# Background conversion's transfers issued from GpSimd, its steps spread by one, and attention's places in a tile changed

## The chip, the cores and the metric

The kernel runs on one core of a Trainium2 chip. The metric is the device time in microseconds of one execution. Three executions of the kernel before gave 1234.53, 1236.09 and 1236.2 us, median 1236.09. A fourth one was taken with the profiler: 1233.03 us, of which 1230.9 us lie between its first and last recorded instruction (the span). All rows below come from that one.

## The reference

Chunked attention with memory tokens, then two feed-forward layers; all in float32.

```python
def _attn_ref(q, k, v, mem_k, mem_v):          # (4, 8, 768, 64), chunks of 32, window 16 back, 8 ahead, 8 memory rows
    for c in range(nc):
        k_full = concat([mem_k, k[l_start:r_end]]); v_full = concat([mem_v, v[l_start:r_end]])
        scores = scale * q_c @ k_full.T
        a = exp(scores - max(scores)); a = a / (sum(a) + 1e-09)
        out[c] = a @ v_full

def _moe_ref(x, w_gate, w_val, w_out, rms_g):   # 3072 tokens, 512 -> 1536 -> 512
    xn = x / sqrt(mean(x * x) + 1e-06) * rms_g
    return (silu(xn @ w_gate) * (xn @ w_val)) @ w_out

def _moe2_ref(x, w_in, w_out):                  # 512 -> 2048 -> 512
    h = x @ w_in
    g = where(h >= 1, h, where(h <= -1, 0, (h + 1) ** 2 / 4))
    return g @ w_out
```

The weights come to the chip as 64-bit floats. The kernel makes float32 of them with integer operations and splits each value into a high and a low part, so that a product is three matmuls: high by high, high by low, low by high.

## The kernel before, in words

The 3072 tokens are six tiles of 512. The program has these stages, by the profile's clock:

- **Start** (to 38 us): attention for the first tokens, in an order written out by hand.
- **Tile 0 of the first layer** (to about 152 us): proj_in (L519) makes gate and value for one block f of 128 hidden columns, out1 (L540) multiplies the block before into ps_y. The first layer's weights are converted beside it, the low parts on GpSimd.
- **Tiles 1 to 3** (to about 530 us): the same loop over f = 0 to 11. Every f has three slots (L689); a slot is one step of attention for later tokens, perhaps one step of preparing the pair, and two steps of a background list `bg`. After this point the order of all instructions on all engines is the program's own.
- **Tiles 4 and 5 as a pair** (about 530 to 720 us): seven products per block instead of eight (product, L807; proj1, L830) in the banks b1 to b4, and out1p (L927). A step of `bg` follows every product, and two follow out1p (L975).
- **Second layer** (720 us to the end): three pairs of tiles, proj2 and out2. No background work is left here.

The list `bg` (L300 to L302) has two kinds of step. w1_steps (L203) makes four sums and differences of quarter blocks of the first layer's weights and stores their high and low parts to DRAM, for the pair. w2_steps (L237) does the conversion for the second layer, in eight groups of four 512-KB blocks a, b, o0 and o1: load_w2 (L232) loads one, c (L245) takes the upper words on ScalarE (ACT), d (L249, three operations of join, L128) makes the float32 on VectorE (DVE), hi (ACT) and lo (DVE) split it, and store (L263) writes it to DRAM; hi_s, lo_s and store_s (L192 to L201) do the same for the sums s1234. Loaded blocks and sums share three buffers in turn (wst, L72), so a load waits until the store that read its buffer has landed. In the kernel before all these loads and stores are issued by ACT: `nc.scalar.dma_start` at L200, L201, L235 and L265. Each engine takes its instructions in order, so a DMA issue that waits holds what stands behind it on the issuing engine.

Attention in tiles 1 to 3 is laid out by `plan2` (L646): which of nine steps of one pair of units stands in which slot; pairs follow each other by 11 slots. A step's name is its kind and its half: s is the scores (matmuls into the bank pair ps_a, then maximum and subtraction on DVE and the exponential on ACT), a the transposes of the exponentials into ps_a and their copy to the tile aT on ACT (part_A, L405), v the product with the values (step_v, L411; DVE then scales it into x_nat), r the normalisation of the rows by the factor rs, which GpSimd raises to a power (part_p, L475), x the transposes of x_nat and their copy on ACT (part_X, L496), whose result xn goes to DRAM as x_d (L506). xn is taken from the same single buffer "aT" that part_A uses.

Of the kernel before, what the change touches and what calls it, by code (L numbers as in the profile page):

```python
# [8 lines left out]
F32 = mybir.dt.float32  # L9
F32R = mybir.dt.float32r  # L10
BF16 = mybir.dt.bfloat16
U32 = mybir.dt.uint32
# [4 lines left out]
P = 128  # L17
# [21 lines left out]
def tile_stream_attention_moe_moe2(  # L39
# [10 lines left out]
    nc = tc.nc  # L50
# [3 lines left out]
    KK = DM // P  # L54
# [8 lines left out]
    att = att_only.enter_context(tc.tile_pool(name="att", bufs=1, side="right"))  # L63
# [119 lines left out]
    def sums(S, a, b, first):  # L183

        if first:
            tt_(out=S[:, 0], in0=b[0], in1=b[1], op=ALU.add)
            tt_(out=S[:, 2], in0=a[0], in1=b[0], op=ALU.subtract)
        else:
            tt_(out=S[:, 1], in0=S[:, 0], in1=a[0], op=ALU.subtract)
            tt_(out=S[:, 3], in0=a[1], in1=S[:, 1], op=ALU.subtract)  # L190

    def hi_s(S, k, h):  # L192
        nc.scalar.activation(h.bitcast(F32R), flat(S[:, k:k + 2]), AF.Copy)

    def lo_s(S, k, h):
        sk = flat(S[:, k:k + 2])
        tt_(out=sk, in0=sk, in1=h.bitcast(F32), op=ALU.subtract)

    def store_s(S, k, h, dp):
        nc.scalar.dma_start(flat(dp[:, 0, 3 + k:5 + k]), h.bitcast(F32))  # L200
        nc.scalar.dma_start(flat(dp[:, 1, 3 + k:5 + k]), flat(S[:, k:k + 2]))  # L201

    def w1_steps(f):  # L203
        g, v = wall[:, 3 * f].bitcast(F32), wall[:, 3 * f + 1].bitcast(F32)
        dp = w1p_d[f]
        st = {}
        half_ = lambda n: [st[n].bitcast(F32)[:, k:k + 256] for k in (0, 256)]

        def whole():
            nc.sync.dma_start(dp[:, :, 0:2].rearrange("p h k c -> p h (k c)"), g)  # L210
            nc.sync.dma_start(dp[:, :, 2], v[:, :, 256:512])
            nc.sync.dma_start(w1o_d[f], wall[:, 3 * f + 2].bitcast(F32))
            for n, w in (("g", g), ("v", v)):
                st[n] = tmp.tile([P, 512], U32, tag="tu", name="w" + n)
                tt_(out=st[n].bitcast(F32), in0=w[:, 0], in1=w[:, 1], op=ALU.add)

        def first():
            st["s"] = wst.tile([P, 4, 256], F32, tag="w64", name="s1234")
            sums(st["s"], half_("g"), half_("v"), True)

        yield whole
        yield first
        yield lambda: sums(st["s"], half_("g"), half_("v"), False)
        yield lambda: hi_s(st["s"], 0, st["g"])
        yield lambda: lo_s(st["s"], 0, st["g"])
        yield lambda: (store_s(st["s"], 0, st["g"], dp), hi_s(st["s"], 2, st["v"]))
        yield lambda: lo_s(st["s"], 2, st["v"])
        yield lambda: store_s(st["s"], 2, st["v"], dp)

    w2raw = {}  # L230

    def load_w2(i):  # L232
        if i < 2 * F2:
            w2raw[i] = wst.tile([P, 1024], U32, tag="w64", name="w64")
            nc.scalar.dma_start(w2raw[i], wts2[i].bitcast(U32))  # L235

    def w2_steps(g):  # L237
        a, b, o0, o1 = 4 * g, 4 * g + 2, 4 * g + 1, 4 * g + 3
        dp, do = w2p_d[g], w2o_d[g]
        f32_, st = {}, {}  # L240
        A = lambda i: [f32_[i].bitcast(F32)[:, k:k + 256] for k in (0, 256)]

        part = lambda i, n: w2raw[i][:, 512 * n:512 * n + 512]

        def c(i):  # L245
            f32_[i] = tmp.tile([P, 512], U32, tag="tu", name="tu")
            nc.scalar.activation(f32_[i].bitcast(F32), words(w2raw[i])[1].bitcast(F32), AF.Copy, scale=2.0 ** -112)

        def d(i):  # L249
            join(f32_[i], w2raw[i])  # L250

        def hi(i, n=0):
            nc.scalar.activation(part(i, 0)[:, n:].bitcast(F32R), f32_[i].bitcast(F32)[:, n:], AF.Copy)

        def lo(i, n=0):
            tt_(
                out=part(i, 1)[:, n:].bitcast(F32),
                in0=f32_[i].bitcast(F32)[:, n:],
                in1=part(i, 0)[:, n:].bitcast(F32),
                op=ALU.subtract,  # L260
            )

        def store(i, dst, n=0):  # L263
            src = w2raw[i].bitcast(F32).rearrange("p (h c) -> p h c", h=2)
            nc.scalar.dma_start(dst, src[:, :, n:])  # L265

        def first():
            st["s"] = wst.tile([P, 4, 256], F32, tag="w64", name="s1234")
            sums(st["s"], A(a), A(b), True)

        if g == 0:
            yield lambda: load_w2(a)
            yield lambda: load_w2(b)
            yield lambda: None
        yield lambda: c(a)
        yield lambda: d(a)
        yield lambda: (hi(a), load_w2(b) if g else None)
        yield lambda: lo(a)
        yield lambda: store(a, dp[:, :, 0:2].rearrange("p h k c -> p h (k c)"))
        yield lambda: None  # L280
        yield lambda: c(b)
        yield lambda: d(b)
        yield lambda: (hi(b, 256), first())
        yield lambda: lo(b, 256)
        yield lambda: (store(b, dp[:, :, 2], 256), sums(st["s"], A(a), A(b), False))
        yield lambda: (hi_s(st["s"], 0, f32_[a]), load_w2(o0))
        yield lambda: lo_s(st["s"], 0, f32_[a])
        yield lambda: (store_s(st["s"], 0, f32_[a], dp), hi_s(st["s"], 2, f32_[b]), load_w2(o1))
        yield lambda: lo_s(st["s"], 2, f32_[b])
        yield lambda: store_s(st["s"], 2, f32_[b], dp)  # L290
        yield lambda: c(o0)
        yield lambda: d(o0)
        yield lambda: (c(o1), load_w2(4 * g + 4))
        yield lambda: (d(o1), hi(o0))
        yield lambda: lo(o0)
        yield lambda: (store(o0, do[:, :, 0]), hi(o1))
        yield lambda: lo(o1)
        yield lambda: store(o1, do[:, :, 1])

    bg = [st for f in range(F1) for st in w1_steps(f)]  # L300
    bg += [st for g in range(G2) for st in w2_steps(g)]
# [27 lines left out]
    x_t = {}  # L329
# [166 lines left out]
    def part_X(pr, blk):  # L496
        t, o = divmod(pr, 2)
        ps = ps_t.pop(("x", pr, blk))
        c0 = (2 * o + blk) * P
        if t < 2:  # L500
            xn = xn_t[t][:, :, c0:c0 + P]
        else:
            xn = att.tile([P, KK, P], F32, tag="aT", name="xn")
        nc.scalar.activation(xn, ps[:, 0, :].rearrange("p (k i) -> p k i", k=KK), AF.Copy)
        if t >= 2:
            nc.sync.dma_start(x_d[t][:, :, c0:c0 + P], xn)  # L506
# [136 lines left out]

    plan2 = {0: "s0", 2: "a0", 3: "v0", 4: "s1", 6: "a1", 7: "v1", 9: "r0", 10: "x0", 12: "x1"}  # L646

    def att_slot(t, s):
        if t == 0:
# [34 lines left out]
    def conv_step(n):  # L684
        for _ in range(n):
            if bg:
                bg.pop()()
# [283 lines left out]
    for f in range(F1):  # L971
        proj1(f)
        if f:
            out1p(0, [f - 1])
        conv_step(2)  # L975
        if f == 6:
            load_y(y_d[0], y_d[1])
    out1p(0, [F1 - 1])
# [117 lines left out]
```

## Time and profile before

| what | value |
|---|---|
| median of three executions | 1236.09 us |
| the profiled execution, its span | 1233.03 us, 1230.9 us |
| TensorE (PE) busy | 1172.4 us, 95% of the span |
| DVE, ACT, GpSimd (POOL) busy | 760.8, 501.9, 86.2 us |
| mean granted TensorE clock | 0.986 of full speed |
| HBM traffic | 225 GB/s over the span |

A page of the profile gives one execution. "Idle before" an instruction is the time in which its engine had nothing running, and the releaser is what ended it. ACTq, SPq and POOLq are the queues from which an engine issues DMAs; an issue is not counted as busy time. The granted clock is the share of full TensorE speed that the throttle allowed.

### The profile page before, as it was taken

Reading aid. Unit: us, or ns where it says so; the run is one execution under the profiler, and the core shown is the slowest. Engines: PE = TensorE matmul, PEld = TensorE weight load, DVE = VectorE, ACT = ScalarE, POOL = GpSimd, SP = SyncE. Lnnn points to the kernel's source line nnn. Section 1 sums busy time; section 2 is a strip of 40 time slices with the busy share of each in tenths; the row PEclk is TensorE's granted clock in tenths of the full one; section 3 lists DMA queues with packets and bytes.
Section 4 is the critical chain, followed back from the end, with each engine's and each line's share of the span. In section 5 each row is a group of like instructions: output and inputs, shape, how many; then the busy total and the mean of one; then the engine's idle time right before and its main releaser. Section 6 shows DMA issues by size and latency. Waiting matters only on the chain.

```text
span 1230.9 us, 19786 instructions
## 1 busy us (share of the span) xinstructions
PE 1172.4 (95%) x7993; PEld 941.1 (76%) x7993; DVE 760.8 (62%) x1256; ACT 501.9 (41%) x830; POOL 86.2 (7%) x75
## 2 busy tenths in 40 slices
PE   6888999998999999988999999999999999999998
PEld 4666777776777778866777788888888888888887
DVE  5898856666546665866766537666267664366630
ACT  4656554445445563533333314334133332233320
POOL 2555510000000000000000000000000000000000
PEclk8989999999999999998999999999999999999999
DMA  8564547777756666498786667657655756565354
GB/s 295 179 196 164 181 157 279 266 276 276 261 179 227 212 202 231 158 348 309 297 338 243 221 220 258 252 192 250 209 200 197 271 194 234 184 235 188 128 183 158
DMA packets 106699, 278.57 MB, mean 226 GB/s; under 512 B 8944, under 2 KB 22256, under 8 KB 100208
## 3 DMA queue, kind: packets, MB, share of 16 engines
q1 hardware_dynamic: 78320, 218.59, 50.8%
q10 hardware_dynamic: 28288, 58.73, 13.2%
q8 instruction: 62, 1.02, 0.3%
q14 instruction: 29, 0.24, 0.1%
HBM read 209.13 MB, written 68.16 MB: 225 GB/s over the span
## 4 chain that ended last, share of the span: by engine, by line
PE 74%; DVE 9%; DMA 9%; ACT 4%; issue 3%; ACTq 1%; POOL 0%; SPq 0%; DVEq 0%; POOLq 0%
PE ps_y L950 7%; PE ps_y L951 7%; PE ps_y L952 7%; PE ps_g L515 5%; PE ps_g L517 5%; PE ps_g L516 5%; PE ps_b L814 5%; PE ps_b L816 5%; PE ps_b L815 5%; PE ps_y L515 4%; PE ps_y L516 4%; PE ps_y L517 4%; PE ps_g L814 3%; PE ps_g L815 3%; PE ps_g L816 3%
## 5 line engine op out<-in xcount | busy, mean ns | idle before, releaser
L515 PE MATMUL ps_g<-xh,wall 128*128 128x512 f32 x384 | 158.4, 412 | 0.0
L517 PE MATMUL ps_g<-xh,wall 128*128 128x512 f32 x384 | 152.7, 398 | 0.0
L516 PE MATMUL ps_g<-xl,wall 128*128 128x512 f32 x384 | 152.6, 397 | 0.0
L950 PE MATMUL ps_y<-wo,wall 128*128 128x512 f32 x324 | 126.2, 389 | 0.3 <-DMA wo<-w2o_d 0.3
L951 PE MATMUL ps_y<-wo,wall 128*128 128x512 f32 x324 | 126.1, 389 | 0.0
L952 PE MATMUL ps_y<-wo,wall 128*128 128x512 f32 x324 | 126.0, 389 | 0.0
L874 ACT ACTIVATE t<-t,half 128x512 f32<-128x512 f32 x96 | 69.0, 720 | 131.5 <-DVE t L873 131.5
L814 PE MATMUL ps_b<-wall 128*128 128x512 f32 x288 | 114.0, 396 | 7.2 <-DVE p L846 7.2
L815 PE MATMUL ps_b<-wall 128*128 128x512 f32 x288 | 113.1, 393 | 0.0
L816 PE MATMUL ps_b<-wall 128*128 128x512 f32 x288 | 113.1, 393 | 0.0
L814 PE MATMUL ps_g<-wall 128*128 128x512 f32 x216 | 85.2, 394 | 7.7 <-ACT p L840 5.6
L888 DVE TENSOR_TENSOR t<-t,ps_g 128x512 f32<-128x512 f32 x24 | 16.5, 688 | 113.5 <-PE ps_g L816 108.8
L517 PEld LDWEIGHTS ps_g<-xh,wall 128*128 128x128 f32 x384 | 72.9, 190 | 17.7
L515 PEld LDWEIGHTS ps_g<-xh,wall 128*128 128x128 f32 x384 | 73.2, 191 | 17.2
L516 PEld LDWEIGHTS ps_g<-xl,wall 128*128 128x128 f32 x384 | 73.3, 191 | 15.4
L816 PE MATMUL ps_g<-wall 128*128 128x512 f32 x216 | 84.7, 392 | 0.0
L815 PE MATMUL ps_g<-wall 128*128 128x512 f32 x216 | 84.6, 392 | 0.0
L515 PE MATMUL ps_y<-hh,wall 128*128 128x512 f32 x192 | 79.1, 412 | 2.6 <-ACT hh L105 2.6
L516 PE MATMUL ps_y<-hl,wall 128*128 128x512 f32 x192 | 76.7, 400 | 0.2 <-DVE hl L106 0.2
L517 PE MATMUL ps_y<-hh,wall 128*128 128x512 f32 x192 | 76.5, 398 | 0.0
L950 PEld LDWEIGHTS ps_y<-wo,wall 128*128 128x128 f32 x324 | 60.8, 188 | 13.4 <-DMA wo<-w2o_d 0.8
L814 PEld LDWEIGHTS ps_b<-wall 128*128 128x128 f32 x288 | 54.7, 190 | 21.0 <-DVE p L846 9.7
(146 smaller groups left out, 2222.0 us busy)
## 6 DMA issues: line engine op xcount, KB each, us to landing
wo<-w2o_d SPq DMA_DIRECT2D x100, 512.0 KB, 4.9
wall<-w2p_d SPq DMA_DIRECT2D x24, 1792.0 KB, 7.2
wall<-w1p_d SPq DMA_DIRECT2D x12, 1792.0 KB, 7.9
w<-in_w_dram SPq DMA_DIRECT2D x36, 512.0 KB, 4.0
w<-in_w_dram ACTq DMA_DIRECT2D x32, 512.0 KB, 4.7
v_in<-in_v_dram SPq DMA_DIRECT2D x48, 260.0 KB, 4.1
k_in<-in_k_dram SPq DMA_DIRECT2D x48, 256.0 KB, 4.3
wo<-w1o_d SPq DMA_DIRECT2D x24, 512.0 KB, 5.7
```

Of the source, the lines that this page charges most:

```text
L515: nc.tensor.matmul(ps, wh, xh, start=start, stop=False)
L516: nc.tensor.matmul(ps, wh, xl, start=False, stop=False)
L517: nc.tensor.matmul(ps, wl, xh, start=False, stop=stop)
L814: nc.tensor.matmul(bank, wh, xh, start=st, stop=False, skip_group_check=True)
L815: nc.tensor.matmul(bank, wh, xl, start=False, stop=False, skip_group_check=True)
L816: nc.tensor.matmul(bank, wl, xh, start=False, stop=kk == 1, skip_group_check=True)
L874: nc.scalar.activation(s, s, AF.Square, scale=0.5, bias=half)
L888: tt(out=u2, in0=a, in1=b2, op=ALU.add)
L950: nc.tensor.matmul(ps_y[m], hi[:, sl], wh, start=b == 0, stop=False)
L951: nc.tensor.matmul(ps_y[m], hi[:, sl], wl, start=False, stop=False)
L952: nc.tensor.matmul(ps_y[m], lo[:, sl], wh, start=False, stop=b == F2 - 1)
```

## The change

Three edits.

1. The transfers of `bg` (store_s, load_w2, store) are issued by GpSimd instead of ACT, and the lists of steps are dealt anew: a step of one engine is mostly followed by a free step before the next engine's, and a store stands in the step of its own lo. w1_steps has 7 steps per block instead of 8, a group of w2_steps 28 instead of 24. In the pair's stage one step follows out1p instead of two.
2. part_X writes xn over the rows' own tile x_nat instead of into a buffer of aT.
3. In plan2 s1 moves from slot 4 to 3, v0 from 3 to 4 and a1 from 6 to 5.

```diff
     def store_s(S, k, h, dp):
-        nc.scalar.dma_start(flat(dp[:, 0, 3 + k:5 + k]), h.bitcast(F32))
-        nc.scalar.dma_start(flat(dp[:, 1, 3 + k:5 + k]), flat(S[:, k:k + 2]))
+        nc.gpsimd.dma_start(flat(dp[:, 0, 3 + k:5 + k]), h.bitcast(F32))
+        nc.gpsimd.dma_start(flat(dp[:, 1, 3 + k:5 + k]), flat(S[:, k:k + 2]))
...
         yield lambda: hi_s(st["s"], 0, st["g"])
-        yield lambda: lo_s(st["s"], 0, st["g"])
-        yield lambda: (store_s(st["s"], 0, st["g"], dp), hi_s(st["s"], 2, st["v"]))
-        yield lambda: lo_s(st["s"], 2, st["v"])
-        yield lambda: store_s(st["s"], 2, st["v"], dp)
+        yield lambda: hi_s(st["s"], 2, st["v"])
+        yield lambda: (lo_s(st["s"], 0, st["g"]), store_s(st["s"], 0, st["g"], dp))
+        yield lambda: (lo_s(st["s"], 2, st["v"]), store_s(st["s"], 2, st["v"], dp))
...
-            nc.scalar.dma_start(w2raw[i], wts2[i].bitcast(U32))
+            nc.gpsimd.dma_start(w2raw[i], wts2[i].bitcast(U32))
...
-            nc.scalar.dma_start(dst, src[:, :, n:])
+            nc.gpsimd.dma_start(dst, src[:, :, n:])
...
         yield lambda: c(a)
+        yield none
         yield lambda: d(a)
-        yield lambda: (hi(a), load_w2(b) if g else None)
-        yield lambda: lo(a)
-        yield lambda: store(a, dp[:, :, 0:2].rearrange("p h k c -> p h (k c)"))
-        yield lambda: None
-        yield lambda: c(b)
+        yield none
+        yield lambda: (c(b), hi(a))
+        yield none
         yield lambda: d(b)
-        yield lambda: (hi(b, 256), first())
-        yield lambda: lo(b, 256)
-        yield lambda: (store(b, dp[:, :, 2], 256), sums(st["s"], A(a), A(b), False))
+        yield lambda: (lo(a), sa())
+        yield lambda: hi(b, 256)
+        yield first
+        yield lambda: (lo(b, 256), sb())
+        yield lambda: sums(st["s"], A(a), A(b), False)
         yield lambda: (hi_s(st["s"], 0, f32_[a]), load_w2(o0))
-        yield lambda: lo_s(st["s"], 0, f32_[a])
-        yield lambda: (store_s(st["s"], 0, f32_[a], dp), hi_s(st["s"], 2, f32_[b]), load_w2(o1))
-        yield lambda: lo_s(st["s"], 2, f32_[b])
-        yield lambda: store_s(st["s"], 2, f32_[b], dp)
+        yield lambda: hi_s(st["s"], 2, f32_[b])
+        yield lambda: (lo_s(st["s"], 0, f32_[a]), store_s(st["s"], 0, f32_[a], dp))
+        yield lambda: (lo_s(st["s"], 2, f32_[b]), store_s(st["s"], 2, f32_[b], dp), load_w2(o1))
+        yield none
         yield lambda: c(o0)
+        yield none
         yield lambda: d(o0)
         yield lambda: (c(o1), load_w2(4 * g + 4))
-        yield lambda: (d(o1), hi(o0))
-        yield lambda: lo(o0)
-        yield lambda: (store(o0, do[:, :, 0]), hi(o1))
-        yield lambda: lo(o1)
-        yield lambda: store(o1, do[:, :, 1])
+        yield lambda: hi(o0)
+        yield lambda: d(o1)
+        yield lambda: (lo(o0), store(o0, do[:, :, 0]))
+        yield lambda: hi(o1)
+        yield none
+        yield lambda: (lo(o1), store(o1, do[:, :, 1]))
+        yield lambda: load_w2(4 * g + 6)
...
-            xn = att.tile([P, KK, P], F32, tag="aT", name="xn")
+            xn = x_t[pr][blk].rearrange("p (k i) -> p k i", k=KK)
...
-    plan2 = {0: "s0", 2: "a0", 3: "v0", 4: "s1", 6: "a1", 7: "v1", 9: "r0", 10: "x0", 12: "x1"}
+    plan2 = {0: "s0", 2: "a0", 3: "s1", 4: "v0", 5: "a1", 7: "v1", 9: "r0", 10: "x0", 12: "x1"}
...
         if f:
             out1p(0, [f - 1])
-        conv_step(2)
+        conv_step(1)
```

How the instructions move is shown at three places. The first is ACT in the pair's stage, at one group of the second layer's weights, before (w is a loaded block, s the sums, tu the float32, p a temporary of the pair, wall a piece of its activations):

```order
L852 ACTIVATE p_5790<-ps_g_100 128x512
L193 ACTIVATE tu<-s_5908 128x512
L235 DMA w_5937<-in_w_dram 128x1024
L856 ACTIVATE p_5794<-p_5794 128x512
L835 ACTIVATE wall<-p_5789 128x512
L835 ACTIVATE wall<-p_5795 128x512
L200 DMA w2p_d_117<-tu 128x512
L201 DMA w2p_d_117<-s_5908 128x512
L193 ACTIVATE tu<-s_5908 128x512
L235 DMA w_5973<-in_w_dram 128x1024
```

The same group on ACT in the change (lines after the diff's place are five higher):

```order
L857 ACTIVATE p_5764<-ps_g_100 128x512
L861 ACTIVATE p_5761<-p_5761 128x512
L840 ACTIVATE wall<-p_5763 128x512
L840 ACTIVATE wall<-p_5762 128x512
L193 ACTIVATE tu<-s_5977 128x512 x2
L845 ACTIVATE p_5765<-ps_g_100 128x512
L246 ACTIVATE tu<-w_6022 128x512
L857 ACTIVATE p_5761<-ps_g_100 128x512
```

No DMA is left between the pair's own operations on ACT; the two copies of the sums stand together. The second place is GpSimd's queue in the change, the same group:

```order
L264 DMA w2p_d_117<-w_5876 256x1x256
L234 DMA w_6022<-in_w_dram 128x1024
L200 DMA w2p_d_117<-tu 128x512
L201 DMA w2p_d_117<-s_5977 128x512
L200 DMA w2p_d_117<-tu 128x512
L201 DMA w2p_d_117<-s_5977 128x512
L234 DMA w_6051<-in_w_dram 128x1024
```

In the kernel before GpSimd has no instruction here. The load of o1 (the last row) now stands behind the four stores of the sums. In tiles 2 and 3 the factor rs stands between such transfers, as here in tile 3:

```order
L234 DMA w_5170<-in_w_dram 128x1024
L264 DMA w2o_d_122<-w_4997 256x1x512
L482 TENSOR_TENSOR rs<-ss,nhalf 128x2
L264 DMA w2o_d_122<-w_5049 256x1x512
L234 DMA w_5292<-in_w_dram 128x1024
```

Before, GpSimd's queue held the eight operations on rs of tiles 1 to 3 one behind the other, with nothing between them. The third place is ACT in tile 2, from the first copy of xn to the next copy of aT, before:

```order
L504 ACTIVATE xn<-ps_a 128x512
L200 DMA w1p_d_138<-wv 128x512
L201 DMA w1p_d_138<-s_3605 128x512
L397 ACT_TABLE_LOAD
L397 ACTIVATE e<-e 128x512
L789 ACT_TABLE_LOAD
L789 ACTIVATE s<-ps_g_100 128x512
L504 ACTIVATE xn<-ps_a 128x512
L193 ACTIVATE wg<-s_3732 128x512
L105 ACTIVATE hh<-s 128x512
L408 ACTIVATE aT<-ps_a 128x512
```

And in the change:

```order
L509 ACTIVATE x_nat<-ps_a 128x512
L246 ACTIVATE tu<-w_3662 128x512
L252 ACTIVATE w_3660<-tu 128x512
L105 ACTIVATE hh<-s 128x512
L413 ACTIVATE aT<-ps_a 128x512
```

The order of xn and aT is the same; xn now lies in x_nat, so the copy to aT no longer follows a write of the same buffer.

## Rows read from the trace of the kernel before

**Rows 1.** The page's first part: span, and busy time by engine.
```profile
span 1230.9 us, 19786 instructions
...
PE 1172.4 (95%) x7993; PEld 941.1 (76%) x7993; DVE 760.8 (62%) x1256; ACT 501.9 (41%) x830; POOL 86.2 (7%) x75
```

**Rows 2.** Windows: stretch, length, busy by engine (instructions), granted clock, DMA share, GB/s.
```profile
152.00:266.00 114.00, 114.00 (x1233) 90.18 (x1232) 69.45 (x134) 58.20 (x96) 7.33 (x7) 1.00 0.69 241
266.00:380.00 114.00, 106.80 (x1139) 83.77 (x1139) 67.18 (x134) 58.22 (x100) 2.75 (x3) 1.00 0.69 238
380.00:487.00 107.00, 104.02 (x1004) 81.73 (x1003) 65.05 (x125) 55.38 (x97) 2.12 (x3) 1.00 0.63 214
487.00:720.00 233.00, 215.07 (x896) 170.94 (x895) 157.46 (x240) 83.15 (x131) 0.00 (x0) 0.97 0.74 273
720.00:890.00 170.00, 169.98 (x749) 140.00 (x748) 96.52 (x151) 54.93 (x83) 0.00 (x0) 1.00 0.65 229
```

**Rows 3.** Waits of PE, 266 to 487: total us, times, longest.
```profile
PE ps_a L418 <- ACT aT L408: 6.6, 6, 1.9
PE ps_a L402 <- ACT xn L504: 1.6, 1, 1.6
```

**Rows 4.** Waits of ACT, 266 to 487.
```profile
ACT aT L408 <- DMA x_d<-xn: 12.6, 5, 4.0
```

**Rows 5.** Chain that ended last, 355 to 372: start, us, what.
```profile
361.02 6.21 DMA x_d<-xn
```

**Rows 6.** Waits of PE, 487 to 720.
```profile
PE ps_b L814 <- DVE p L846: 7.2, 4, 5.1
PE ps_g L814 <- ACT p L840: 5.6, 3, 2.8
PE ps_y L515 <- ACT hh L105: 2.6, 1, 2.6
```

**Rows 7.** Waits of ACT, 487 to 720.
```profile
ACT tu L247 <- DMA w<-in_w_dram: 29.0, 10, 8.0
...
ACT p L840 <- DMA w2p_d<-s: 6.6, 1, 6.6
```

**Rows 8.** Timeline of ACT, 556 to 567: start, us, instruction, [idle before, releaser].
```profile
556.77 0.33 ACTq L235 DMA_DIRECT2D w<-in_w_dram  x1
557.15 0.63 ACT L856 ACTIVATE p<-p 128x512 f32<-128x512 f32 x1 [3.12 <-DMA w2p_d<-w]
...
566.19 0.66 ACT L247 ACTIVATE tu<-w 128x512 f32<-128x512 f32 x1 [3.77 <-DMA w<-in_w_dram]
```

**Rows 9.** Windows of 10 us in the pair's stage, columns as in rows 2.
```profile
560.00:570.00 10.00, 4.87 (x20) 3.69 (x20) 4.83 (x8) 2.57 (x4) 0.00 (x0) 0.93 0.83 304
570.00:580.00 10.00, 10.00 (x34) 7.98 (x33) 6.87 (x12) 4.03 (x7) 0.00 (x0) 0.73 0.73 259
...
660.00:670.00 10.00, 10.00 (x46) 8.22 (x45) 5.14 (x8) 2.30 (x4) 0.00 (x0) 1.00 0.64 236
```

**Rows 10.** DMA issues, 487 to 720: times, KB each, median us to landing.
```profile
w<-in_w_dram ACTq DMA_DIRECT2D x16, 512.0 KB, 5.3
...
w2p_d<-s ACTq DMA_DIRECT2D x8, 256.0 KB, 8.6
```

**Rows 11.** Timeline of SP, issues of y_d in tiles 2 and 3.
```profile
301.99 0.33 SPq L549 DMA_DIRECT2D y_d<-ys  x1
...
428.44 0.33 SPq L549 DMA_DIRECT2D y_d<-ys  x1
```

**Rows 12.** Groups by line, whole span, GpSimd: count, busy us, mean ns, idle before.
```profile
L106 POOL TENSOR_TENSOR wall<-tu,wall 128x512 fp32r<-128x512 f32 x36 | 50.3, 1401 | 56.9 <-ACT wall L105 56.8
```

**Rows 13.** Groups by line and shape, 38 to 152, DVE, columns as in rows 12.
```profile
L137 DVE SCALAR_TENSOR_TENSOR tu<-w,tu 128x512 uint32<-128x512 uint32 x32 | 35.5, 1112 | 0.7
```

**Rows 14.** The same, 487 to 720.
```profile
L137 DVE SCALAR_TENSOR_TENSOR tu<-w,tu 128x512 uint32<-128x512 uint32 x18 | 12.5, 692 | 0.6
...
L131 DVE TENSOR_SCALAR tu<-tu 128x512 uint32<-128x512 uint32 x18 | 7.6, 422 | 15.0 <-ACT tu L247 14.9
```

More of the change, by code (lines that the diff above doesn't have):

```diff
@@ L269, in first @@
             sums(st["s"], A(a), A(b), True)
+        sa, sb = (lambda: (store(a, dp[:, :, 0:2].rearrange("p h k c -> p h (k c)"))), lambda: store(b, dp[:, :, 2], 256))
+        none = lambda: None
         if g == 0:
-            yield lambda: load_w2(a)
-            yield lambda: load_w2(b)
-            yield lambda: None
+            yield lambda: (load_w2(a), load_w2(b))
+            yield none
+            yield none
         yield lambda: c(a)
+        yield none
         yield lambda: d(a)
-        yield lambda: (hi(a), load_w2(b) if g else None)
@@ L278, in w2_steps @@
-        yield lambda: lo(a)
-        yield lambda: store(a, dp[:, :, 0:2].rearrange("p h k c -> p h (k c)"))
-        yield lambda: None
-        yield lambda: c(b)
-        yield lambda: d(b)
-        yield lambda: (hi(b, 256), first())
-        yield lambda: lo(b, 256)
-        yield lambda: (store(b, dp[:, :, 2], 256), sums(st["s"], A(a), A(b), False))
+        yield none
+        yield lambda: (c(b), hi(a))
+        yield none
+        yield lambda: d(b)
+        yield lambda: (lo(a), sa())
@@ L291, in w2_steps @@
+        yield lambda: (lo_s(st["s"], 0, f32_[a]), store_s(st["s"], 0, f32_[a], dp))
+        yield lambda: (lo_s(st["s"], 2, f32_[b]), store_s(st["s"], 2, f32_[b], dp), load_w2(o1))
+        yield none
         yield lambda: c(o0)
+        yield none
         yield lambda: d(o0)
         yield lambda: (c(o1), load_w2(4 * g + 4))
-        yield lambda: (d(o1), hi(o0))
-        yield lambda: lo(o0)
-        yield lambda: (store(o0, do[:, :, 0]), hi(o1))
-        yield lambda: lo(o1)
-        yield lambda: store(o1, do[:, :, 1])
+        yield lambda: hi(o0)
@@ L300, in tile_stream_attention_moe_moe2 @@
+        yield lambda: d(o1)
+        yield lambda: (lo(o0), store(o0, do[:, :, 0]))
+        yield lambda: hi(o1)
+        yield none
+        yield lambda: (lo(o1), store(o1, do[:, :, 1]))
+        yield lambda: load_w2(4 * g + 6)
     bg = [st for f in range(F1) for st in w1_steps(f)]
```

## The prediction

> **What bounds the kernel now.** I read the page first. PE is busy 95% of the span and no other engine over 62% [rows 1], so time can come only from stretches where PE waits or runs at the lower clock. The windows by stage show where these are [rows 2]: from 152 to 266 us PE has no idle time, from 266 to 380 it idles 114.0 - 106.8 = 7.2 us, from 380 to 487 3.0 us, from 487 to 720 17.9 us, and in 720 to 890 nothing again (170.0 against 169.98). The granted clock is 1.00 except in the 487 to 720 stretch, where it is 0.97: 0.03 x 233 = 7.0 us of TensorE's time. So the stages with background work hold 7.2 + 3.0 + 17.9 + 7.0 = 35.1 us that could go. That is the most the change can bring; the second layer is out of its reach.
>
> Next the waits of PE in these stages. In tiles 2 and 3 most is one kind: v waits for the copy to aT, 6.6 us in six times, and 1.6 us for a copy of xn [rows 3]. In the last stretch PE waits 7.2 us for DVE's sum u4 (L846), 5.6 us for ACT's copy of b1 (L840), 2.6 us for ACT's hh [rows 6]. Both engines have free time there (DVE 157 of 233 us busy, ACT 83), so the question is what held them. ACT's own waits answer: 29.0 us in ten times for a load of a weight block, and 6.6 us before a plain PSUM copy until a store of s had landed [rows 7]. The timeline shows such a pair [rows 8]. At 557.15 ACT starts a Silu after 3.12 us of waiting for a store to land, because the load issued at 556.77 stood ahead of it and needed that store's buffer. That load reached its reader at 566.19, 9.4 us later, and ACT waited again, 3.77 us. DVE's join stood behind that, u4 behind the join, and PE behind u4: the window 560 to 570 has 4.87 us of PE work, and the one after it a clock of 0.73, with PE busy throughout [rows 9]. The clock falls after the stall and costs a second time.
>
> **Lengths of a step.** Undisturbed, 46 matmuls take 10 us [rows 9], so a product (6) takes 1.3 us and a block of proj1 and out1p (42 + 12) 11.7 us. That block had 9 background steps, 1.3 us each, and has 8 now, 1.46 us each. In tiles 1 to 3 a tile takes 428.44 - 301.99 = 126.5 us [rows 11], a slot 126.5 / 36 = 3.5 us, a step 1.76 us. The list has 12 x 7 + 3 + 8 x 28 = 311 steps (it had 12 x 8 + 3 + 8 x 24 = 291), and 3 x 72 + 12 x 8 = 312 places: it just fits, and nothing is left to be done in one go at its end.
>
> **Edit 2, xn in the rows' tile.** ACT waits 12.6 us in five times before aT until x_d has landed [rows 4]; one such store took 6.21 us and stands whole on the chain [rows 5]. This wait goes. What is late next: DVE writes x_nat again at the next pair's v0, three slots or 10.5 us after the second store; 6.21 us is hidden in that, with 4 us to spare. **Edit 3** has no wait of its own to remove: s1 stands one slot behind a0 as v0 did, and must wait for the same copy before it overwrites ps_a. It gives v0 and v1 two slots each behind their copies. k and q for s1 are loaded three slots ahead instead of four, 10.5 us; I count nothing for this, and if a load came late it would cost what exceeds that. Together: of the 6.6 us I take 5 us as gone. The 1.6 us behind xn sits at the tile's boundary, where DVE splits the next tile; it stays, with most of the rest. Bounds: 0 if another ACT wait takes aT's place, 10.2 if all goes. **Term 1: -5 us.**
>
> **Edit 1, what leaves ACT.** 144 transfers (12 x 4 stores, 8 x 4 loads, 8 x 8 stores) leave ACT. Their issue, 0.33 us by the row [rows 8], is hidden beside ACT's free time and I count nothing for it. What counts is their waiting. The 6.6 us and 3.12 us [rows 7, 8] are of that kind and go. The waits for loads go only if loads come earlier. The tightest chain is: store of a block, load into its buffer, c of that load. A store of s lands after 8.6 us, a load after 5.3 us, medians [rows 10]: 13.9 us. Before, store b, load o1 and c(o1) stood in steps 11, 14 and 19: 8 x 1.3 = 10.4 us, and the sums to the next a 9 steps, 11.7 us. Neither fits. Now they are steps 11, 16 and 21, 10 x 1.46 = 14.6 us, and for the next a 13 steps, 19 us. They fit if GpSimd adds little. Further, d follows c two steps later (before: one) in three of four blocks; 2.9 us of delay then reach ACT but not DVE.
>
> **What GpSimd adds.** The trace has no DMA issued by GpSimd. Below, an issue costs 0.33 us as on ACT [rows 8]; above, I take GpSimd's own operation over 128x512 elements, 1.4 us [rows 12], and choose 1 us, nearer the upper row because it is the same engine. Two of them in a chain make 13.9 + 2 = 15.9 us against 14.6: 1.3 us late in the tightest chain, inside the 2.9. Its own queue: load o1 stands behind four stores, 4 us more than its place says, when these wait for nothing. That is the transfer I expect to see late. rs now stands between transfers; it is asked for two slots (7 us) later by r0, and a queue held for a landing store (8.6 us) could cost DVE 2 us once or twice, not more.
>
> So of the 17.9 us I leave 5 us, for a load that takes 9.4 us [rows 8] instead of 5.3 in one group in three. **Term 2: -13 us.** The clock followed the stalls; with under a third of these I leave 2 of the 7.0 us. **Term 3: -5 us.** Sum: -23 us on 1233.0 us, the profiled execution's own time, so 1210. The median of the runs is 1236.1, 3.1 us more; I give times on that basis: **1213 us**. Its own range runs from 1204 (32 us gained) to 1221 (15 us gained).
>
> **A rule against edit 1.** The rows put a load's landing at 5.3 us and its issue at 0.33 us [rows 8, 10]. The Trainium skill, "DMA: Bandwidth & Descriptors", section "Issuing engines are not separate DMA queues", says that transfers run on the same 16 DMA engines whoever starts them, and that another issuer saves only the time of issuing. By that rule alone the waits for loads stay, which is the first rival. No run here has shown transfers of GpSimd yet.
>
> **Rivals.** *The loads land as late as before.* The DMA share of 0.74 in the last stretch [rows 2] and landings well over a quiet one speak for it; that the same bytes are spread over more time (28 steps of 1.46 us = 41 us a group, was 24 x 1.3 = 31) speaks against. Then only waits of the buffer kind go. Of ACT's waits they are 6.6 + 3.1 against 29.0 for loads, a quarter: (17.9 + 7.0) / 4 = 6 us. With term 1 the gain is 11: 1225 us.
>
> *GpSimd's issuing slows DVE.* While GpSimd works beside it (38 to 152 us) an operation of join takes 1112 ns instead of 692 [rows 13, 14]: 1.6 times. A join and u4 take 0.42 + 3 x 0.69 = 2.5 us in the last stretch, just under the two products (2.6 us) that PE leaves between writing b3 and needing it again. At 1.6 times it is 4.0 us, 1.4 us too much, for 18 joins 25 us, and 7.0 / 17.9 of that again for the clock: 35 us on top of 1213, 1248 us, slower than before. It decides where a stretched join and u4 pass 2.6 us. Against: rows 13 show operations that read SBUF on GpSimd, and issuing a transfer is none. The Trainium skill, "SBUF — State Buffer", section "Who interferes with whom", has a DVE instruction with two SBUF inputs contend with a GpSimd instruction that reads SBUF, not with one that only writes. By that rule this rival falls.
>
> *GpSimd issues too slowly.* A block of w1_steps issues 4 transfers in 7 x 1.76 = 12.3 us, 3.1 us each. At 4 us each the list runs 3.7 us late per block, 12 x 3.7 = 44 us, through sums that wait for a buffer on DVE: 1213 + 44 = 1257 us. Against: 2.2 times the longer row of GpSimd.
>
> *Nothing comes of it:* one wait takes the other's place everywhere, 1236 us.
>
> **Chances.** A measurement of this kernel tells 0.2%, 2.5 us, from no change. Forecast 0.62, late loads 0.19, nothing 0.05, slowed DVE 0.10, slow issuing 0.04. So faster 0.81, same 0.05, slower 0.14. The range takes in the forecast's, the late loads and no change: 1203 to 1237; the two slower rivals and a little below it, under 0.2 together, are left out.
>
> **What would show it.** Right: no DMA on ACT's queue before the second layer; the wait of aT for x_d gone; PE idle under 6 us from 266 to 487 and about 5 in the pair's stage, clock there near 0.99; ACT's waits for loads below 15 us; DVE's L137 at 0.69 us. Wrong: L137 above 0.8 us beside GpSimd's transfers; loads that land over 8 us in the median with ACT still waiting 25 us for them; GpSimd transfers over 3 us apart with nothing to wait for; a new wait of PE behind r0 or behind k.

## The result, and the profile after

The kernel before takes 1236.08 us in the median of four runs (1234.53 to 1236.2), the changed one 1224.88 us (1222.18 to 1226.81). The ratio is 0.9911, with a 95% interval of 0.9887 to 0.9935: **faster by 11 us, less than half of the 23 us forecast.** The profiled execution of the changed kernel took 1226.4 us, among the longer of its runs, so the two profiles differ by 6.6 us only.

Here a stall is a stretch in which PE stands idle, a landing the time from a transfer's issue to its end. The page's first part and the windows by stage of the changed kernel (columns as in [rows 2]):

```profile
span 1224.6 us, 19878 instructions
PE 1175.7 (96%) x7993; PEld 945.4 (77%) x7993; DVE 758.4 (62%) x1256; ACT 497.0 (41%) x830; POOL 169.3 (14%) x219
```

```profile
152.00:266.00 114.00, 112.56 (x1166) 88.90 (x1165) 71.19 (x139) 58.83 (x101) 25.53 (x40) 1.00 0.72 252
266.00:380.00 114.00, 111.60 (x1240) 87.39 (x1246) 70.75 (x138) 59.50 (x105) 19.45 (x33) 1.00 0.70 237
380.00:487.00 107.00, 104.69 (x1002) 83.03 (x990) 59.49 (x116) 51.05 (x91) 20.35 (x33) 0.98 0.61 209
487.00:530.00 43.00, 43.00 (x187) 34.71 (x186) 32.59 (x46) 18.77 (x28) 8.21 (x14) 1.00 0.51 174
530.00:720.00 190.00, 177.38 (x730) 141.39 (x729) 123.87 (x195) 62.98 (x103) 22.83 (x38) 0.95 0.80 297
```

Against [rows 2]: from 266 to 487 PE idles 2.4 + 2.3 = 4.7 us where it was 10.2, but tile 1, which had none, idles 1.4 us, and a clock of 0.98 costs 0.02 x 107 = 2.1 us in tile 3. The kernel before has in the last two windows:

```profile
487.00:530.00 43.00, 40.20 (x168) 31.86 (x167) 33.18 (x47) 19.28 (x28) 0.00 (x0) 0.97 0.58 210
530.00:720.00 190.00, 174.88 (x729) 139.08 (x729) 124.28 (x194) 63.87 (x103) 0.00 (x0) 0.97 0.77 287
```

The 2.8 us of 487 to 530 and the lowered clock there are gone. The pair's stage from 530 on keeps 12.6 us of idle time (15.1 before), and its clock is lower than before, 0.95 against 0.97: 9.5 us against 5.7. From 487 to 720, where 18 us were forecast, 17.9 - 12.6 = 5.3 us of idle time are gained and 9.5 - 7.0 = 2.5 us lost again by the clock.

PE's waits from 487 to 720, where [rows 6] show three names, are now nearly one, and so are ACT's behind them (same columns):

```profile
PE ps_g L819 <- ACT p L845: 11.6, 3, 5.2
PE ps_b L819 <- DVE p L851: 0.7, 2, 0.6
```

```profile
ACT tu L246 <- DMA w<-in_w_dram: 44.7, 9, 9.5
```

ACT waits longer for its loads than before, 44.7 us against 29.0 [rows 7]; its 6.6 us for a store are gone. L845 is ACT's copy of b1; it stands behind c (L246) in ACT's queue. The three stalls of PE, from its timeline, with two matmuls between the first and the second:

```profile
536.65 0.80 PE L819 MATMUL ps_g<-wall 128*128 128x512 f32 x1 [5.22 <-ACT p L845]
...
540.35 0.63 PE L820 MATMUL ps_b<-wall 128*128 128x512 f32 x1
...
544.00 0.39 PE L820 MATMUL ps_g<-wall 128*128 128x512 f32 x1
...
565.21 0.50 PE L819 MATMUL ps_g<-wall 128*128 128x512 f32 x1 [3.51 <-ACT p L845]
...
659.04 0.79 PE L819 MATMUL ps_g<-wall 128*128 128x512 f32 x1 [2.86 <-ACT p L845]
```

After the first stall the granted clock is 0.50, the lower of its two levels (1.2 and 2.4 GHz), and it is 1.00 again from 544 to 550:

```profile
537.00:541.00 4.00, 3.82 (x9) 2.54 (x9) 3.38 (x7) 0.77 (x2) 0.56 (x1) 0.50 0.94 311
```

The work of ACT and of GpSimd that belongs to the second stall, from their timelines:

```profile
563.50 0.66 ACT L246 ACTIVATE tu<-w 128x512 f32<-128x512 f32 x1 [7.43 <-DMA w<-in_w_dram]
564.06 0.61 ACT L252 ACTIVATE w<-tu 128x512 fp32r<-128x512 f32 x1
564.58 0.57 ACT L845 ACTIVATE p<-ps_g 128x512 f32<-128x512 f32 x1
```

```profile
527.48 0.56 POOL L234 DMA_DIRECT2D w<-in_w_dram  x1
539.16 0.56 POOL L234 DMA_DIRECT2D w<-in_w_dram  x1 [11.12 <-DMA w2p_d<-s]
544.48 0.69 POOL L264 DMA_DIRECT2D w2o_d<-w  x1 [4.77 <-DVE w L255]
548.32 0.71 POOL L264 DMA_DIRECT2D w2o_d<-w  x1 [3.15 <-DVE w L255]
555.65 0.57 POOL L234 DMA_DIRECT2D w<-in_w_dram  x1 [6.63 <-DVE p L867]
```

The store of o0 is issued at 544.48. The load of the next group's b takes the same buffer (three rotate) and goes out at 555.65, 11.2 us later; GpSimd had nothing else to do from 549.03 on. Its c runs at 563.50, 7.9 us after that. The chain is 19.0 us long; the list gives it 9 steps (store in step 24 of 28, c of b in step 5 of the next group), 9 x 1.46 = 13.1 us. The last row names DVE as the releaser, but the store of o0 took 10.8 us from its issue to its landing, so it landed at 555.3 us, and the load went out at 555.65. The DMA issues of 544 to 545:

```profile
w2o_d<-w POOLq DMA_DIRECT2D x1, 512.0 KB, 10.8
```

SP starts a 1.8 MB load of wp (the pair's weights for one block) at 543.97, in the same half microsecond as that store. The row joins two issues; the second goes out at 553.50, 2.2 us ahead of the load of b:

```profile
543.97 9.85 SPq L728 DMA_DIRECT2D wall<-w1p_d  x2
```

Two things the prediction feared did not come, by the instructions of one line, 487 to 720:

```profile
L137 DVE SCALAR_TENSOR_TENSOR tu<-w,tu x18: 691/692/693, 492.6 to 684.2; 128x512 uint32<-128x512 uint32 x18
```

```profile
L234 POOL DMA_DIRECT2D w<-in_w_dram x17: 548/561/582, 489.3 to 674.2; - x17
```

DVE's join takes 692 ns as before [rows 14], and the issue of a load on GpSimd 0.56 us.

### The profile page after: what moved, and what is told of

It is laid out like the page before. It is cut to its first block, busy times and chain, and to the rows that moved or that the text cites. A ratio compares the mean times of both kernels' runs of the same rounds, so it can differ in the third digit from the quotient of the medians.

```text
span 1224.6 us, 19878 instructions
## 1 busy us (share of the span) xinstructions
PE 1175.7 (96%) x7993; PEld 945.4 (77%) x7993; DVE 758.4 (62%) x1256; ACT 497.0 (41%) x830; POOL 169.3 (14%) x219
## 5 line engine op out<-in xcount | busy, mean ns | idle before, releaser
L819 PE MATMUL ps_g<-wall 128*128 128x512 f32 x216 | 85.9, 398 | 11.6 <-ACT p L845 11.6
L955 PEld LDWEIGHTS ps_y<-wo,wall 128*128 128x128 f32 x324 | 60.8, 188 | 12.9 <-DMA wo<-w2o_d 0.2
L956 PEld LDWEIGHTS ps_y<-wo,wall 128*128 128x128 f32 x324 | 60.8, 188 | 12.6
```

The lines of the kernel that those rows point to most:

```text
L819: nc.tensor.matmul(bank, wh, xh, start=st, stop=False, skip_group_check=True)
L955: nc.tensor.matmul(ps_y[m], hi[:, sl], wh, start=b == 0, stop=False)
L956: nc.tensor.matmul(ps_y[m], hi[:, sl], wl, start=False, stop=False)
```

## The experiments

**First four runs: which edit gives what, and is it the wp loads?** My theory T after reading the trace was that the stalls come from transfers that share the DMA engines with wp's loads. Rivals: the buffers, GpSimd's queue, the steps. The kernel before was measured anew beside each group of runs: 1235.67 us beside these four, 1236.72 beside the next four, 1237.13 beside the last four. Gains over the kernel before are differences of medians against these; the ratio, with its interval, weighs the single runs otherwise and can differ from them by 1 to 2 us. Gains over the changed kernel go by its 1224.88 us, so they are uncertain by the 1.5 us by which the kernel before differs from group to group.

*Edit 1 alone* (before, with the first three parts of the diff and conv_step(1); attention as before).

> The kernel before with edit 1 alone: GpSimd issues the conversion's transfers and the engines' steps have the new free steps; attention is as before. Theory T (the stalls of the pair's stage come from loads and stores that share the DMA engines with the 1.8 MB loads of wp, so their lead of some 7 us doesn't do): the pair's stage from 530 to 720 us idles about 12 us as in the changed kernel, with three stalls of 3 to 5 us behind L845, so edit 1 gives only the 2.8 us and the clock of 487 to 530 back: 4 to 6 us below the kernel before, about 1231. The tiles 2 and 3 keep their 10 us of idle time and the 12.6 us of waiting for x_d. Rival (edit 3's slots disturb the conversion list, and edit 1 alone would have worked): the pair's stage idles under 5 us and the time is about 1218. Rival (edit 1 is worth nothing, all comes from edits 2 and 3): within 2.5 us of the kernel before.

Measured: 1225.01 us, ratio 0.9926 (0.9896 to 0.9956). That is 10.7 us (9.1 by the ratio), within the intervals all that the whole change gives; theory T's 1231 allowed too little for it, and its rivals (1218, or nothing) are out. The pair's stage is as T said (12.0 us idle, 11.0 of it behind L845). But tiles 2 and 3 idle 4.9 us, as in the changed kernel, without edits 2 and 3. ACT's wait for x_d is still there, and hardly anybody waits for it; the waits of ACT and of PE from 266 to 487:

```profile
ACT aT L413 <- DMA x_d<-xn: 10.6, 5, 4.2
```

```profile
PE ps_a L423 <- ACT aT L413: 1.4, 2, 0.9
```

*Edits 2 and 3 alone.*

```
-            xn = att.tile([P, KK, P], F32, tag="aT", name="xn")
+            xn = x_t[pr][blk].rearrange("p (k i) -> p k i", k=KK)
...
-    plan2 = {0: "s0", 2: "a0", 3: "v0", 4: "s1", 6: "a1", 7: "v1", 9: "r0", 10: "x0", 12: "x1"}
+    plan2 = {0: "s0", 2: "a0", 3: "s1", 4: "v0", 5: "a1", 7: "v1", 9: "r0", 10: "x0", 12: "x1"}
```

> The kernel before with edits 2 and 3 alone: xn in the rows' tile, the new table of slots; the conversion's transfers stay on ACT with the old steps. If the 5.5 us that tiles 2 and 3 idle less in the changed kernel come from these two edits and the two halves add up: 5 to 7 us below the kernel before, about 1230, idle time of about 5 us from 266 to 487 and the old 17.9 us from 487 to 720. Rival (the conversion's transfers on ACT had held aT too, so edit 1 is needed for it): tiles 2 and 3 still idle 8 us or more, the time within 2.5 us of the kernel before.

Measured: 1233.84 us, ratio 0.9985 (0.9965 to 1.0006): 1.8 us that can't be told from nothing. The wait for x_d is gone, the idle time of 266 to 487 falls to 7.1 us only, and 4.2 of these are one new stall. The timelines of PE and ACT:

```profile
414.69 1.00 PE L402 MATMUL ps_a<-ident,e 128*128 128x128 f32 x4 [4.23 <-DVE x_nat L445]
```

```profile
405.61 2.07 ACTq L201 DMA_DIRECT2D w2p_d<-s  x1
407.73 0.67 ACT L247 ACTIVATE tu<-w 128x512 f32<-128x512 f32 x1 [1.92 <-issue]
408.31 2.18 ACT L311 ACTIVATE xh<-xn 128x512 fp32r<-128x512 f32 x4
```

ACT's queue stands 2.07 us in the issue of a store; behind it come c, the split of x, DVE's xl and last x_nat. Another wait in ACT's queue has taken the place of the one removed.

*The new steps, but ACT issues.*

```
-        nc.gpsimd.dma_start(flat(dp[:, 0, 3 + k:5 + k]), h.bitcast(F32))
+        nc.scalar.dma_start(flat(dp[:, 0, 3 + k:5 + k]), h.bitcast(F32))
...
```

> The changed kernel with its new steps, but the conversion's transfers are issued by ACT again. Tells the issuer from the steps. Theory T: the landings are the same whoever issues, so ACT's waits for loads stay near 45 us in nine waits; on top ACT waits itself for stores to land before it can issue into their buffers, 7 to 11 us each at some places: slower than the changed kernel by 3 to 15 us, 1228 to 1240. Rival (the free steps do it all, the issuer nothing): within 2.5 us of the changed kernel. Rival (GpSimd's own queue delays the loads): faster than the changed kernel, below 1222, and landings shorter than 5.9 us in the median.

Measured: 1227.55 us, ratio 0.9925 (0.9896 to 0.9953): the changed kernel without its new issuer, 2.7 us above its median and inside both intervals. The waits for w fall to 26.0 us, others for stores (14.4 and 6.0) stand beside them. So the steps do most, the issuer little. In the profiles the pair's stage shows no help from GpSimd: from 487 to 720 PE idles 10.5 us here and 12.6 in the changed kernel, and the first of its three stalls, at 536 us, isn't in this run; tiles 2 and 3 idle 7.6 us against 4.7. The landings show no direction that goes with the issuer: with the same steps and attention a load of w takes 7.5 us in the median from ACT here and 5.9 from GpSimd in the changed kernel, but 5.3 from ACT in the kernel before and 7.6 from GpSimd in the run of the issuer alone (below).

*Half of wp* (the low halves of the pair's weights aren't loaded).

```
-            nc.sync.dma_start(wp[:, n % 2].bitcast(F32), src)
+            nc.sync.dma_start(wp[:, n % 2, 0].bitcast(F32), src[:, 0])
```

> The changed kernel, but each load of wp brings only the high halves of the pair's weights, 896 KB instead of 1792 KB; the low halves are left out and stale. So the DMA engines have 10.8 MB less to carry in the pair's stage. Theory T (shared DMA engines): the conversion's loads and stores beside it land in 4 to 6 us instead of 8 to 11, the three stalls behind L845 go, the idle time of 530 to 720 falls from 12.6 us to under 4 and the clock there goes to 0.99: 12 to 17 us below the changed kernel, about 1210. Rival (the buffers: a load must wait for the store of the buffer three back, whatever else is on the engines; or GpSimd's queue): the stalls stay within a third, 8 us or more of idle time, and less than 5 us gained.

Measured: 1209.30 us, ratio 0.9792 (0.975 to 0.9834), 15.6 us below the changed kernel, as T said. Window of the pair's stage and DMA issues (487 to 720):

```profile
530.00:720.00 190.00, 187.03 (x808) 152.22 (x807) 126.73 (x199) 65.56 (x107) 24.37 (x41) 0.99 0.73 256
```

```profile
w<-in_w_dram POOLq DMA_DIRECT2D x17, 512.0 KB, 4.3
...
w2p_d<-s POOLq DMA_DIRECT2D x10, 256.0 KB, 4.9
```

In the changed kernel these are 5.9 and 6.3 us, in the run of edit 1 alone, with the same pair's stage, 7.7 and 7.4: both runs lie above this one. The bytes beside them make the landings long. The first stall is gone too. The load of o0 whose c made ACT wait 9.55 us ahead of that stall lands in 4.5 us where it took 10.6; c follows without a wait, and one stall of 2.8 us, at 543.74, is left. This load in the changed kernel (issues of 524 to 525), and here (526.5 to 527):

```profile
w<-in_w_dram POOLq DMA_DIRECT2D x1, 512.0 KB, 10.6
```

```profile
w<-in_w_dram POOLq DMA_DIRECT2D x1, 512.0 KB, 4.5
```

That does not yet say that only the bytes can be helped.

**Next four runs: buffers, pieces, both, and the issuer by itself.**

*Five buffers* (the sums use the buffer e of the pair's pool, every fourth load a 4 KB tile of that pool).

```
-            w2raw[i] = wst.tile([P, 1024], U32, tag="w64", name="w64")
+            if "pool" in m2:
+                m2["loads"] = m2.get("loads", 0) + 1
+            pool_ = m2["pool"] if m2.get("loads", 0) % 4 == 1 else wst
+            w2raw[i] = pool_.tile([P, 1024], U32, tag="w64", name="w64")
...
-            st["s"] = wst.tile([P, 4, 256], F32, tag="w64", name="s1234")
+            if "e" in m2:
+                st["s"] = m2["e"].rearrange("p a (b c) -> p (a b) c", b=2)
+            else:
+                st["s"] = wst.tile([P, 4, 256], F32, tag="w64", name="s1234")
```

> The changed kernel with more room for the conversion in the pair's stage: the sums get a buffer of their own and every fourth load a 4 KB tile that lies free there, so that four blocks and the sums share five buffers instead of three. The loads and their places in the list are the same. Theory T (shared DMA engines alone): a load can issue without waiting for the store of the block three back, but it lands as late beside a load of wp; of the 12.6 us of idle time in 530 to 720 about half stays: 0 to 8 us below the changed kernel. Rival (buffers: the store must land first, 8 to 11 us, and only this makes the loads late): GpSimd's waits for w2p_d<-s (20.7 us) go, the three stalls go, idle time under 4 us, clock 0.99: 12 to 17 us below the changed kernel, as with half of wp.

Measured: **1211.63 us**, ratio 0.9807 (0.9788 to 0.9825), 13.3 us below the changed kernel with all bytes loaded. The rival's side. Windows, GpSimd and ACT:

```profile
530.00:720.00 190.00, 184.31 (x791) 149.59 (x790) 125.37 (x197) 64.86 (x106) 22.50 (x38) 0.98 0.85 313
```

```profile
549.33 0.71 POOL L267 DMA_DIRECT2D w2o_d<-w  x1 [3.28 <-DVE w L258]
550.00 0.60 POOL L237 DMA_DIRECT2D w<-in_w_dram  x1
```

```profile
556.98 0.66 ACT L249 ACTIVATE tu<-w 128x512 f32<-128x512 f32 x1
```

The load goes out right behind the stores, waits for none of them, and c finds its data. The second and third stall are gone; a median landing of 7.0 us, longer than in the changed kernel, does no harm. The first stall (5.3 us at 537.7) stays.

*wp in pieces.*

```
         product(f, b4, 5, 3, True)
+        load_wp(f + 2, 3, 6)
...
         product(f, b1, 1, 4, False)
+        load_wp(f + 2, 0, 2)
...
         product(f, b3, 6, 5, False)
+        load_wp(f + 2, 6, 7)
...
-        load_wp(f + 2)
+        load_wp(f + 2, 2, 3)
```

> The changed kernel with the load of wp for the block after next in four pieces (3, 2, 1 and 1 of its 7 columns), each issued as soon as the product that reads these columns is done, instead of whole at the block's end. The same bytes. Theory T: the burst is spread over the block, loads and stores of the conversion land between its pieces, in 4 to 7 us: the stalls shrink to 6 us or less, 4 to 12 us below the changed kernel. Rival (the bytes of the whole stage bind, 297 GB/s in the mean, however they are spread): idle time of 10 us or more, less than 3 us gained.

Measured: 1214.20 us, ratio 0.9831 (0.9804 to 0.9859), 10.7 us below the changed kernel. The same chain, at GpSimd and ACT:

```profile
543.27 0.69 POOL L264 DMA_DIRECT2D w2o_d<-w  x1 [5.28 <-DVE w L255]
547.30 0.71 POOL L264 DMA_DIRECT2D w2o_d<-w  x1 [3.35 <-DVE w L255]
551.27 0.57 POOL L234 DMA_DIRECT2D w<-in_w_dram  x1 [3.26 <-DVE tu L137]
```

```profile
557.90 0.67 ACT L246 ACTIVATE tu<-w 128x512 f32<-128x512 f32 x1 [2.85 <-DMA w<-in_w_dram]
```

Store to load 8.0 us (was 11.2), load to c 6.6 (was 7.9): 14.6 us in all, and the 2.9 us that ACT still waits don't reach PE.

*Both.* Five buffers and the four pieces.

> The changed kernel with five buffers and wp in pieces. If bursts and buffers each make a part of the lateness, this is the fastest: idle time in 530 to 720 under 4 us, clock 0.99, about 1210 us, as with half of wp. If one of the two alone does it, no faster than that one by more than 2.5 us.

Measured: 1212.27 us, ratio 0.9813 (0.9794 to 0.9833), no faster than five buffers alone: the two cut the same chain, and the first stall, 5.4 us, is in this run too.

*The issuer alone* (before, with nc.gpsimd in place of nc.scalar in the conversion's four transfers).

> The kernel before, with its steps and its attention, only that GpSimd issues the conversion's transfers. Tells the issuer from the free steps; the run with ACT as the issuer and the new steps has given 8 us against the kernel before. If the free steps give nearly all: within 3 us of the kernel before, ACT's waits for loads at 29 to 40 us, its waits before joins on DVE (L253, 15 us in tiles 2 and 3) unchanged. Rival (either half is enough, since both free ACT): 6 to 10 us below the kernel before, about 1227. Rival (GpSimd's issuing costs by itself, and the steps make up for it): slower than before by 3 us or more.

Measured: 1234.50 us, ratio 0.9976 (0.9957 to 0.9995): 2.2 us. ACT's wait before L253 in tiles 2 and 3 (14.9 us before) stands at 14.6 us, 10.2 of them with no releaser named. From 487 to 720 ACT waits for no store any more, but its wait for loads grows to 49.3 us, and PE idles 21.6 us in the profiled run where it was 17.9: by itself the new issuer does the pair's stage no good.

```profile
487.00:720.00 233.00, 211.43 (x888) 168.54 (x887) 155.97 (x240) 81.96 (x131) 29.91 (x50) 0.96 0.73 271
```

**Last four runs.** *A late start:* no background step in the first four products of the pair's stage, on top of five buffers.

```
-        conv_step(1)
+        if n or x > 3:
+            conv_step(1)
```

> The changed kernel with five buffers, and with no background step in the first four products of the pair's stage, so that c(o0) of the running group comes 4 steps or some 6 us later; the list's last steps are done in one go at its end. One stall of 5.3 us is left in the run with five buffers: at 536 us, where ACT waits 9.6 us for a load that waited itself for a store and shares the DMA engines with both first loads of wp. If that is a matter of lead alone (theory: store, load and c must fit into the steps between them): the stall goes, idle time of 530 to 720 under 2 us, clock 0.99 or more, 5 to 9 us below the run with five buffers, about 1204. Rival (the later steps run into the end of the list or into loads of w2o that come too late): no more than 2.5 us below it, or slower.

Measured: 1218.05 us, ratio 0.9846 (0.9815 to 0.9876), 6.4 us above five buffers: the rival. The stall at 537 shrinks to 1.3 us, but all later steps move against SP's loads, the load of w takes 10.5 us in the median of 487 to 720 (7.0 with five buffers alone), and the rest of the list runs in one go at its end. Two new stalls come, of 3.9 and 2.9 us; which of these moves makes each isn't shown. PE's timeline, and its wait from 680 to 700:

```profile
636.77 0.80 PE L825 MATMUL ps_g<-wall 128*128 128x512 f32 x1 [3.87 <-ACT p L852]
```

```profile
PE ps_y L526 <- ACT wall L847: 2.9, 1, 2.9
```

*The steps alone* (ACT issues, attention as before).

> The kernel before with the new free steps alone: ACT issues the transfers as before, attention as before. With the issuer alone at 2 us, edits 2 and 3 alone at 2 us and edit 1 whole at 10.7 us, the steps alone should give 6 to 9 us, about 1228, if the parts add up; ACT's waits before L253 for DVE's join in tiles 2 and 3 (14.9 us) go, PE's waits for aT (6.6 us) go to 3 us or less though ACT still waits some 11 us for x_d. Rival (the steps need GpSimd as issuer, since ACT's own transfers then hold it): less than 4 us below the kernel before.

Measured: 1229.47 us, ratio 0.9932 (0.9904 to 0.996): 7.7 us. PE's waits for aT from 266 to 487 fall from 6.6 to 2.0 us, though ACT waits 10.0 us for x_d. The waits before the split copies (L252) do not all go: 9.5 us stand there under DVE's lo (L255). In the run of edit 1 alone, where no store that waits for lo is in ACT's queue, 0.4 us are left. From 487 to 720 PE idles 14.4 us (17.9 before). The parts add up within the intervals: 2.2 and 7.7 us make 9.9, and edit 1 whole gave 10.7.

*wp's second load cut.*

```
-    load_wp(1)
+    load_wp(1, 0, 1)
+    load_wp(1, 3, 5)
...
         load_wo(i)
+    load_wp(1, 5, 7)
+    load_wp(1, 1, 3)
```

> The run with five buffers, with the load of wp for the pair's second block cut: 3 of its 7 columns are loaded where all were, the other 4 (1 MB) only behind the first four loads of wo, some 15 us later. This takes 1 MB out of the burst in which the load that stalls ACT at 526 to 536 us lands. Theory (landings lengthen with the bytes beside them): it lands 2 to 3 us sooner, the one stall left (5.3 us) shrinks to 3 us or less, and the time is 2 to 5 us below the run with five buffers. Rival: the late columns come after their products (PE waits for wall<-w1p_d), or the burst only moves onto the next load: no change within 2.5 us, or slower.

Measured: 1212.92 us, ratio 0.9814 (0.9781 to 0.9848), no change: the stall of 5.3 us falls into four of 0.8 to 1.7 us, one of them the late columns themselves, and the rival holds for the time. PE's timeline and the window:

```profile
546.50 0.47 PE L826 MATMUL ps_b<-wall 128*128 128x512 f32 x1 [1.66 <-DMA wall<-w1p_d]
```

```profile
530.00:720.00 190.00, 185.10 (x803) 149.74 (x802) 126.46 (x199) 64.82 (x106) 22.41 (x38) 1.00 0.86 318
```

*Five buffers again*, beside that run on the same chip.

> The run with five buffers once more, beside the one before on the same chip: 1211 us, ratio to the kernel before 0.979 to 0.983, idle time of 530 to 720 near 5.7 us with one stall.

Measured: 1212.44 us, ratio 0.9799 (0.9775 to 0.9823); one stall, of 4.3 us, and 4.9 us of idle time. Five buffers is the best version here that loads every byte, 25 us below the kernel before and about 13 below the changed one.

## Why the prediction was wrong in size

The direction and the place were right, the size was not. In the kernel before, four of PE's waits for aT come right behind an ACT operation that had waited for x_d:

```profile
290.93 0.86 PE L418 MATMUL ps_a<-v_in,aT 64*32 64x65 f32 x64 [1.33 <-ACT aT L408]
329.52 0.86 PE L418 MATMUL ps_a<-v_in,aT 64*32 64x65 f32 x64 [0.97 <-ACT aT L408]
367.98 0.86 PE L418 MATMUL ps_a<-v_in,aT 64*32 64x65 f32 x64 [1.89 <-ACT aT L408]
405.46 0.86 PE L418 MATMUL ps_a<-v_in,aT 64*32 64x65 f32 x64 [0.64 <-ACT aT L408]
```

In the profiled pair the terms measure:

- **Term 1, forecast -5, measured about -2.** The idle time of 266 to 487 fell by 5.5 us as written, but 1.4 us of idle time in tile 1 and 2.1 us of clock in tile 3 were not in the sum. And it came from the wrong edit. The step that failed is "ACT waits 12.6 us in five times ... This wait goes", taken as time that PE gains by edits 2 and 3, while edit 1 was given nothing in these tiles. In the timeline of before the wait stands in front of PE only four times (the rows above), for 4.8 of its 6.6 us of waiting. With edits 2 and 3 alone PE's waits for aT do go, but a new stall of 4.2 us behind ACT's queue comes in, and 1.8 us are gained, or nothing: the prediction's own bound, "0 if another ACT wait takes aT's place". With edit 1 alone, and the wait for x_d left in place, PE's waits for aT fall from 6.6 to 1.4 us and the idle time to 4.9 us, near the 4.7 of all three edits. That 5.5 us came near the 5 written is luck.
- **Term 2, forecast -13, measured -5.3** (17.9 to 12.6 us). The step that failed is "They fit if GpSimd adds little", a chain sized with the medians 8.6 and 5.3 us. GpSimd did add little (0.56 us for the issue of a load, 0.69 for a store's, where 1 us was taken). The landings were mis-sized: stores issued beside a load of wp took up to 11 us until the next load could go, the load behind them 7.9 us. And the tightest chain was another than the one costed: store of o0, load of the next b, c, 9 steps or 13.1 us, needed 19.0 us. The text had a row with 9.4 us in hand and allowed it once in three groups for the load; it allowed nothing for the store ahead of it. (Its three of four blocks in which d follows c two steps later are all four; that doesn't change the sum.) "The 6.6 us and 3.12 us ... are of that kind and go" held for ACT's own list only: GpSimd now waits for such stores (20.7 us for those of s), ACT still waits for the loads behind them, and with the issuer alone PE idles 21.6 us in this stage against 17.9.
- **Term 3, forecast -5, measured +2.5** (7.0 to 9.5 us in 487 to 720): the clock follows stalls, as written, and three large ones remained. After the stall of 5.2 us a matmul takes 0.63 us at a granted clock of 0.50, and 0.39 us at 1.00; the window of 530 to 720 has 0.95 in the changed kernel, 0.96 in the run of edit 1 alone and 0.98 where one stall is left. The term hung on term 2.

Together -4.8 of the 6.6 us between the two profiles. Where the rest lies isn't shown; stages that no edit touches differ by as much: in the window of 38 to 152 us, whose code is the same in all these kernels, PE is busy 97.3 to 100.8 us from run to run.

The rivals: *the loads land as late as before* names the time (1225) and is right that the loads stay late, but the time is partly luck: its 11 us had 5 from edit 2, which by itself gives 1.8 or nothing, and 6 from the pair's stage, where the profiles differ by 5.3 - 2.5 = 2.8. *GpSimd's issuing slows DVE* is refuted by 692 ns. By the rule of the Trainium skill, "SBUF — State Buffer", section "Who interferes with whom", a DVE instruction with two SBUF inputs contends with a GpSimd instruction that reads SBUF. The prediction took an issue for no such read, and the trace agrees. *GpSimd issues too slowly* falls with 0.56 to 0.69 us. On the rule against edit 1, from the Trainium skill, "DMA: Bandwidth & Descriptors", section "Issuing engines are not separate DMA queues": the run with the issuer alone agrees in the main, 2.2 us. The steps, the other half of edit 1, are worth 7.7 us by themselves.

That the chain is the cause of the second and third stall in the pair's stage is shown from three sides: fewer bytes, two more buffers, or the same bytes spread out each take the second and third stall away, and two of them together give no more than one. The first stall, at 536 us, hangs on the bytes beside its load as well: with half of wp that load lands in 4.5 instead of 10.6 us and the stall is gone. No run with all bytes turned this into time: the stall breaks up with 1 MB less in its burst and shrinks with a later start, and neither gained anything. Why it is not there when ACT issues the same steps isn't shown. The cost of attention's new table apart from xn's tile was not tried.

## What to carry to other kernels

Size a chain of store, load and use by the landings at the moment when the largest other load runs, not by medians over the stage, and follow every buffer of the rotation to the store that frees it. If it doesn't fit, more buffers in places that lie free may be worth more (13 us here for two, 2 us for the issuer) than moving the issue to another engine. A wait with a large sum in one engine's list is worth only what the engine behind it waits at those very places: 12.6 us of ACT's time held PE for 1.3 + 1.0 + 1.9 + 0.6 = 4.8 us here, and when it was taken away, another wait in the same queue took 4.2 us. To move a waiting transfer to another engine frees the first engine's queue, but doesn't make the transfer earlier: with the issuer alone ACT waited 49.3 us for loads in the pair's stage, 29.0 before.

## What was not expected of the hardware

- Transfers issued close together can all land late: of those that GpSimd issued from 524.79 to 527.5 us, behind a load of wp issued at 523.20, the load landed after 10.6 us and the four stores after 11.6 to 11.9, all between 535 and 539 us; the next load, which needed one of these stores, went out at 539.16.
- The length of a landing follows the bytes beside it: with wp's loads halved the load of w takes 4.3 us and the store of s 4.9 us in the median of 487 to 720, where the two runs with whole loads and the same code there have 5.9 and 7.7, and 6.3 and 7.4.
- The issue of a load costs GpSimd 0.56 us where ACT took 0.33 [rows 8], and leaves DVE's join at 692 ns.
